# One distance mask for the first four blocks, added through sloped unit matrices; the scheduler's start values and dates set anew

## Chip, cores and metric

The kernel runs on one core of one Trainium2 chip. The metric is the device time of one execution in microseconds; the time before is the median of three runs.

## What is computed

Attention over 4 batches, 8 heads, 768 positions and 64 dimensions, with a window of `n_local` keys, `n_global` keys seen by all, and a bias that falls with the distance by a slope of its own for each head; then a feed-forward part on 3072 tokens.

```python
scores = scale * q @ k.T
keep = is_global | is_local            # rel = row - column; 0 <= rel < n_local, or column < n_global
dist = where(is_global & ~is_local, n_local, abs(rel))
slopes = 2.0 ** (-8.0 * (arange(H) + 1) / H)
scores = where(keep, scores - slopes[:, None, None] * dist, -1e9)
a = softmax(scores)
x = (a @ v)                            # [3072, 512]
h = x @ w_in                           # 512 x 2048
out = (h * sigmoid(1.702 * h)) @ w_out # 2048 x 512
```

With 8 heads the slope of head h is 2 to the power -(h+1).

## The kernel before

The 3072 rows are 24 blocks of 128. The first four (one of each batch, `first`) see only their own keys; the others (`unit`, four units of two heads each) see their own block, the one before and the global keys. For a first block TensorE writes the scores `s` (four heads to a tile), adds to each head its mask, and DVE takes the maxima of the rows, `top`. The maxima are transposed (`aux`), copied to `mT`, and the scores are made a second time with rows and columns exchanged (`sT`): the product, the mask, and the maxima. ACT takes the exponential (`pt`), TensorE multiplies by the values (`pv`), DVE divides (`x`), TensorE turns the result (`tx`), and ACT and DVE split it into two halves of 16 bits (`xT`).

The mask of distances is built on DVE (`distances`, `own`, `other`) in `mk`: part 2 for the first blocks, parts 0 and 1 for the units. `slopes` multiplies it by the slope of each head into `mm`. TensorE adds a mask by a product with the unit matrix `id16`: in `s`, `id16` is the loaded matrix and `mm[:, h, 2]` streams; in `sT`, `mm[:, h, 2]` is loaded and `id16` streams.

The weights come in 16 loads of 1 MB (`ws`, three buffers) and are turned into two halves of 16 bits by two passes on ACT and three on DVE each (lines 420 to 426). The feed-forward part makes `h` from `xT` and `w`, `t` and `g` on ACT and DVE, and `y` from `g`; from the third pair of blocks on, products of a faster scheme write `pa` and `pb`.

All work is a list of tasks. `Work.order` plays them on five engines with a cost of its own for each task, takes at each point the ready task with the earliest due date, and so fixes the order in which each engine gets its instructions. `NUDGE` adds to the due date of the tasks with a given tag; where TensorE would stand idle in the first 50 us, the scheduler puts in a product on `idle`, here called a filler. On the chip each engine runs its instructions in that order, and waits at each until its inputs are there. The queue SP issues nearly all transfers in its own order; a load into a buffer that is still read waits, and so do those behind it. `QKover` holds the keys of the blocks that block 4 follows: SP turns them in one transfer from `qk16over` and copies them in two more.

Of the kernel before, what the change touches and what calls it, by code (L numbers as in the profile page):

```python
# [11 lines left out]
BF16 = mybir.dt.bfloat16  # L12
# [16 lines left out]

NUDGE = {"M2": -8.8, "T2": 21.9, "T3": 11.2, "block1": 2, "block10u2": -2.7, "block10u2l": -0.5,  # L30
# [48 lines left out]
LAT = 0.2  # L79
MM128, MM256, MM512, MM64, FP128, FP65, TURN = 0.056, 0.109, 0.216, 0.029, 0.264, 0.21, 0.11  # L80
# [43 lines left out]
class Work:  # L124
# [15 lines left out]
    def order(self):  # L140
# [21 lines left out]
        dma, now, done = 2.5, 0.0, []  # L162
        worked, spared = 0.6, 0
# [82 lines left out]
def kernel(  # L246
# [48 lines left out]
    id16 = const.tile([P, P], BF16, name="id16")  # L295
# [38 lines left out]
    mm = const.tile([P, H, 3, P], BF16, name="mm")  # L334
# [9 lines left out]
    def distances(e):  # L344

        nc.vector.tensor_copy(flt()[:, 0:2], ints())
        nc.vector.tensor_copy(id16, ident)
# [31 lines left out]
    def slopes(e, js, hs=range(H)):  # L379
# [9 lines left out]
    m0 = add({"DVE": 1.6}, distances, [m0], [ints, flt, mk], -4.0)  # L389
    cs = Buf(r_pv, [P, 2], F32, "cs")  # L390
# [10 lines left out]
    M2 = [add({"DVE": 0.41, "ACT": 0.6}, lambda e, f=f: slopes(e, slice(0, 2), range(2 * f, 2 * f + 2)), [m2], [mk], 34.0) for f in range(4)]  # L401
# [5 lines left out]
    def weights(s, u):  # L407
# [8 lines left out]
        t0 = add({"SP": 2.75}, lambda e: load_weights(nc, ws(), w_in, w_out, s, u), bufs=[ws])  # L416
# [32 lines left out]
    def load(n, raw, parts=(0, 1, 2)):  # L449
        b, i = place(n)  # L450
        return [add({"SP": 1.2 if n < 2 and 2 not in parts else 1.35}, lambda e, z=z: nc.sync.dma_start(
            raw()[:, z], (q, k, v)[z][b, :, i * P:(i + 1) * P, :].rearrange("h p d -> p h d")), bufs=[raw]) for z in parts]
# [911 lines left out]
```

## Time and profile before

| | us |
|---|---|
| median of three runs (588.32 to 590.07) | 589.75 |
| span of the profiled execution | 587.0 |
| PE busy | 578.1 |
| DVE busy | 497.0 |
| ACT busy | 461.4 |

The span goes from the first to the last instruction of one execution. PE is TensorE's products, DVE VectorE, ACT ScalarE, POOL GpSimd, SP the queue of transfers. A product's end is modelled, so a product of 128 columns reads 0.22 us although the next starts 0.055 us after it: the step from one start to the next is what it costs in a row of products. Where a row gives a wait, it is in brackets with what ended it.

### The profile page before, as it was taken

Reading aid. Unit: us, or ns where it says so; the run is one execution under the profiler, and the core shown is the slowest. Engines: PE = TensorE matmul, PEld = TensorE weight load, DVE = VectorE, ACT = ScalarE, POOL = GpSimd, SP = SyncE. Lnnn points to the kernel's source line nnn. Section 1 sums busy time; section 2 is a strip of 40 time slices with the busy share of each in tenths; the row PEclk is TensorE's granted clock in tenths of the full one; section 3 lists DMA queues with packets and bytes.
Section 4 is the critical chain, followed back from the end, with each engine's and each line's share of the span. In section 5 each row is a group of like instructions: output and inputs, shape, how many; then the busy total and the mean of one; then the engine's idle time right before and its main releaser. Section 6 shows DMA issues by size and latency. Waiting matters only on the chain.

```text
span 587.0 us, 16903 instructions
## 1 busy us (share of the span) xinstructions
PE 578.1 (98%) x6744; PEld 435.0 (74%) x6744; DVE 497.0 (85%) x1180; ACT 461.4 (79%) x1086; POOL 3.7 (1%) x14
## 2 busy tenths in 40 slices
PE   8999999999999999999999999999999999999996
PEld 5886666777678678778679767777777866876896
DVE  7898999999999999888899699889889878775462
ACT  6678899898678979888798798798987878874351
POOL 2000000000000000000000000000000000000000
PEclk9999999999999999999999999999999999999999
DMA  9988998988767887989999998999998899981101
GB/s 267 315 262 213 301 239 234 214 186 154 174 138 154 145 150 156 222 163 203 222 182 179 213 222 210 218 201 184 243 204 197 196 204 232 192 179 25 30 2 41
DMA packets 268265, 109.57 MB, mean 187 GB/s; under 512 B 249300, under 2 KB 249812, under 8 KB 268180
## 3 DMA queue, kind: packets, MB, share of 16 engines
q1 hardware_dynamic: 268032, 108.30, 83.3%
q8 instruction: 54, 0.88, 0.6%
q14 instruction: 31, 0.25, 0.1%
q10 hardware_dynamic: 148, 0.13, 0.1%
HBM read 57.67 MB, written 6.29 MB: 109 GB/s over the span
## 4 chain that ended last, share of the span: by engine, by line
PE 82%; DVE 6%; DMA 6%; ACT 4%; issue 2%; SPq 0%; POOL 0%; DVEq 0%; ACTq 0%; POOLq 0%
PE y L969 35%; PE pa L901 15%; PE pb L901 11%; PE h L861 7%; PE s L599 5%; DMA QKover<-qk16over 2%; PE pv L630 1%; PE pv L632 1%; PE pv L631 1%; PE sT L692 1%; DMA ws<-in_moe_w_out_dram 1%; DMA ws_00again<-in_moe_w_in_dram 1%; DMA xT<-x 1%; PE idle L1147 1%; PE pv L704 1%
## 5 line engine op out<-in xcount | busy, mean ns | idle before, releaser
L969 PE MATMUL y<-w,g 128*128 128x512 f16 (+1 forms) x1248 | 265.1, 363 | 0.3
L969 PEld LDWEIGHTS <-g 128*128 128x128 f16 x1248 | 118.0, 98 | 106.6 <-DVE g L873 1.4
L901 PEld LDWEIGHTS <-w 128*128 128x128 f16 x1728 | 101.4, 98 | 3.9
L615 ACT ACTIVATE p<-p,NM 128x232 f32<-128x232 f32 x160 | 76.3, 479 | 8.9 <-DVE NM L605 8.6
L901 PEld LDWEIGHTS <-T 128*128 128x128 f16 x1296 | 76.8, 98 | 5.2 <-issue 0.2
L861 PE MATMUL h<-xT,w 128*128 128x256 f16 x576 | 67.2, 273 | 0.2 <-DVE t L871 0.2
L605 DVE CUSTOM_DVE_ANT_0 p<-s,mm 128x232 f32<-128x232 f32 x160 | 57.5, 393 | 9.3 <-PE s L599 9.0
L861 PEld LDWEIGHTS <-w 128*128 128x128 f16 x576 | 55.4, 98 | 8.1 <-DVE t L871 0.3
L942 DVE SCALAR_TENSOR_TENSOR g<-t,g 128x512 f16<-128x512 f32 x72 | 49.0, 686 | 11.2 <-ACT g L941 10.9
L620 DVE TENSOR_TENSOR hl<-p,hl 128x464 f16<-128x464 f32 x80 | 50.8, 635 | 6.2 <-ACT hl L619 5.9
L941 ACT ACTIVATE g<-t 128x512 f16<-128x512 f32 x72 | 44.9, 628 | 12.1 <-PE y L969 8.2
L933 ACT ACTIVATE t<-h 128x512 f32<-128x512 f32 (+1 forms) x72 | 35.8, 517 | 17.8 <-DVE h L909 16.0
L619 ACT CAST hl<-p 128x464 f16<-128x464 f32 x80 | 46.0, 574 | 2.3 <-DMA pt<-hl 0.9
L909 DVE TENSOR_TENSOR h<-pb,h 128x256 f32<-128x256 f32 x72 | 28.4, 418 | 19.4 <-PE pb L901 17.8
L901 PE MATMUL pa<-xS,T 128*128 128x128 f16 x648 | 44.8, 219 | 0.0
L599 PEld LDWEIGHTS <-QK 128*128 128x128 f16 x640 | 36.5, 98 | 6.0 <-DVE NM L605 1.9
L934 DVE SCALAR_TENSOR_TENSOR t<-t,h 128x512 f32<-128x512 f32 (+1 forms) x72 | 38.4, 551 | 2.2 <-ACT t L933 2.0
L599 PE MATMUL s<-QK 128*128 128x128 f16 x320 | 38.2, 219 | 0.0
L901 PE MATMUL pa<-xT,w 128*128 128x128 f16 x540 | 37.5, 219 | 0.0
L901 PE MATMUL pb<-xS,w 128*128 128x128 f16 x540 | 37.5, 219 | 0.0
L632 PE MATMUL pv<-VR,pt 128*128 128x64 f16 x288 | 34.5, 193 | 0.0
L631 PE MATMUL pv<-VR,pt 128*128 128x64 f16 x288 | 34.5, 193 | 0.0
(186 smaller groups left out, 1031.2 us busy)
## 6 DMA issues: line engine op xcount, KB each, us to landing
ws<-in_moe_w_in_dram SPq DMA_DIRECT2D x8, 1024.0 KB
ws<-in_moe_w_out_dram SPq DMA_DIRECT2D x8, 1024.0 KB, 5.6
raw<-in_q_dram SPq DMA_DIRECT2D x24, 256.0 KB, 3.7
raw<-in_k_dram SPq DMA_DIRECT2D x24, 256.0 KB, 4.8
QK<-QK SPq DMA_DIRECT2D x40, 128.0 KB, 5.5
raw<-in_v_dram SPq DMA_DIRECT2D x20, 256.0 KB, 3.1
out_dram<-yo SPq DMA_DIRECT2D x20, 256.0 KB
ws_00again<-in_moe_w_in_dram SPq DMA_DIRECT2D x8, 512.0 KB, 4.0
```

The lines of the kernel that those rows point to most:

```text
L599: nc.tensor.matmul(sp()[:, j, lo:hi], d["QK"]()[:, 0, h, :], K[:, 1 + z, h, P - (hi - lo):], start=(z == 0), stop=(z == 1), skip_group_che ...
L605: nc.vector.tensor_tensor_reduce(out=pr()[:, j, :], in0=sp()[:, j, :], in1=m, scale=-1.0 / SC, scalar=3.0e38, op0=ALU.add, op1=ALU.min, ac ...
L615: ex.append(add({"ACT": 0.473}, lambda e, j=j: nc.scalar.activation(pr()[:, j, :], pr()[:, j, :], AF.Exp, bias=NM[:, n, hs[j]:hs[j] + 1], ...
L619: t4 = add({"ACT": 0.5}, lambda e: nc.scalar.copy(hl()[:, 0, :, SKIP:], pr()), ex, [pr, hl])
L620: t5 = add({"DVE": 0.55}, lambda e: nc.vector.tensor_sub(hl()[:, 1, :, SKIP:], pr(), hl()[:, 0, :, SKIP:]), [t4], [pr, hl])
L631: nc.tensor.matmul(o, ph, V[:, 1, h], start=False, stop=False, skip_group_check=True)
L632: nc.tensor.matmul(o, pl, V[:, 0, h], start=False, stop=(s == ns - 1), skip_group_check=True)
L861: nc.tensor.matmul(ph()[:, fi, :], w1(s, cc, z, fi), X[:, y, cc, :], start=(j + cc == 0), stop=(j == 2 and cc == NCC - 1))
L901: nc.tensor.matmul(o()[:, fi], w, x()[:, y * NCC + 2 * k + cc, t], start=(first and fi + j + cc == 0), stop=(last and j + cc == 3), skip_g ...
L941: t4 = add({"ACT": 0.53}, lambda e, g=g, tt=tt: nc.scalar.mul(g()[:, 0], tt(), SG / (SX * SW)), u, [tt, g])
L942: t5 = add({"DVE": 0.61}, lambda e, g=g, tt=tt: nc.vector.scalar_tensor_tensor(g()[:, 1], tt(), SG / (SX * SW), g()[:, 0], ALU.mult, ALU.s ...
L969: nc.tensor.matmul(y(), part(zg, f), w2(s, z, f % 2)[:, m], start=(begin and f + j == 0), stop=(end and j == 2 and f == 2 * len(steps) - 1 ...
```

## The change

The mask of the first blocks is kept once, unsloped: `own16` is a copy of `mk[:, 2]` in bf16, and `idh[:, h]` is the unit matrix times the slope of head h. In `s` the loaded matrix is now `idh[:, h]` and `own16` streams; in `sT` `own16` is loaded and the four unit matrices of a half stream in one product of 512 columns. Since the column of the unit matrix that adds the maxima now carries the smallest slope, `mT` is divided by it. `mm` loses its third part, `id16` is gone. The diagonals need only the unit matrix, which POOL makes.

```diff
+    own16 = const.tile([P, P], BF16, name="own16")
+    idh = const.tile([P, H, P], BF16, name="idh")
...
-    M1 = [add({"DVE": 0.61}, lambda e, f=f: slopes(e, slice(2, 3), range(4 * f, 4 * f + 4)), [m1], [mk]) for f in range(2)]
+    M1 = [*D1, add({"DVE": 0.2, "ACT": 0.22}, lambda e: (nc.scalar.copy if e == "ACT" else nc.vector.tensor_copy)(own16, mk()[:, 2]),
+                   [m1], [mk])]
...
+    def diagonals(e, hs):
         for h in hs:
-            f = SC * 2.0 ** -(h + 1)
             if e == "ACT":
-                nc.scalar.mul(mm[:, h, js], mk()[:, js], f)
+                nc.scalar.mul(idh[:, h], ident, slope(h))
             else:
-                nc.vector.tensor_scalar(mm[:, h, js], mk()[:, js], f, None, ALU.mult)
+                nc.vector.tensor_scalar(idh[:, h], ident, slope(h), None, ALU.mult)
...
+    D1 = [add({"DVE": 0.6, "ACT": 0.9}, lambda e, f=f: diagonals(e, range(4 * f, 4 * f + 4)), want=2.0 + f) for f in range(2)]
...
-                    nc.tensor.matmul(sp()[:, j], id16, mm[:, h, 2], start=False, stop=True, skip_group_check=True)
+                    nc.tensor.matmul(sp()[:, j], idh[:, h], own16, start=False, stop=True, skip_group_check=True)
...
-                    nc.tensor.matmul(o, mm[:, h, 2], id16, start=False, stop=False, skip_group_check=True)
-                    nc.tensor.matmul(o, id16[:, h:h + 1].broadcast_to([P, P]), mT, start=False, stop=True, skip_group_check=True)
+                nc.tensor.matmul(sT(), own16, idh[:, hs], start=False, stop=False, skip_group_check=True)
+                for j in range(4):
+                    nc.tensor.matmul(sT()[:, j], idh[:, H - 1, 4 * f + j:4 * f + j + 1].broadcast_to([P, P]), mT,
+                                     start=False, stop=(j == 3), skip_group_check=True)
```

The scheduler starts with other values: the transfers' first free time and TensorE's first filler, the cost of the first loads (1.0 in place of 1.2), of the first weight load and of a `turned` task.

```diff
+DMA0, PE0 = 1.85, 1.3
...
-        dma, now, done = 2.5, 0.0, []
-        worked, spared = 0.6, 0
+        dma, now, done = DMA0, 0.0, []
+        worked, spared = PE0, 0
...
-        t0 = add({"SP": 2.75}, lambda e: load_weights(nc, ws(), w_in, w_out, s, u), bufs=[ws])
+        t0 = add({"SP": 2.75 if s or u else 3.5}, lambda e: load_weights(nc, ws(), w_in, w_out, s, u), bufs=[ws])
```

And `NUDGE` is another table, with about twice as many entries; two of its old and new ones:

```diff
-NUDGE = {"M2": -8.8, "T2": 21.9, "T3": 11.2, "block1": 2, "block10u2": -2.7, "block10u2l": -0.5,
+NUDGE = {"M1": 2.8, "T0": 14.2, "T1": 5.3, "T3": -8.5, "again": 1.3, "againl": -2.1, "block0": 4.5,
```

So the order changes on every engine from the first instructions to the last. At the start, TensorE gets 13 fillers instead of 16, seven of them ahead of the first transposes instead of ten, and the scores of blocks 0 and 1 stand in a row. Three places follow.

The start on DVE, from the first memsets to the mask of the first blocks (`flt`, `mk`: distances; `one`, `cnt`: counts). Before:

```order
L503 MEMSET VF_124 128x8
L346 CAST flt<-ints 128x256
L347 CAST id_84<-ident 128x128
L348 TENSOR_SCALAR mk<-flt 128x128
...
L353 CAST cf<-ci 1x4
...
L356 SCALAR_TENSOR_TENSOR one<-one,cf 1x2
L393 COPY cnt<-cs 128x2
...
L372 SCALAR_TENSOR_TENSOR mk<-flt,cnt,mk 128x128
L385 TENSOR_SCALAR mm<-mk 128x128 x8
```

Now:

```order
L415 TENSOR_SCALAR idh<-ident 128x128 x8
...
L375 CAST flt<-ints 128x256
L376 TENSOR_SCALAR mk<-flt 128x128
...
L381 CAST cf<-ci 1x4
...
L384 SCALAR_TENSOR_TENSOR one<-one,cf 1x2
L531 TENSOR_SCALAR QZ_136<-tq_0_177 64x512
L431 COPY cnt<-cs 128x2
...
L400 SCALAR_TENSOR_TENSOR mk<-flt,cnt,mk 128x128
```

Eight products with slopes moved from behind the mask to ahead of the distances, and half of a QZ came to DVE. The same stretch on ACT, where `hl` holds the turned keys; before:

```order
L492 ACTIVATE QZ_116<-tq_0_171 64x512 x2
L492 ACTIVATE hl_97<-tq_1_188 128x512
L492 ACTIVATE QZ_131<-tq_0_208 64x512 x2
L383 ACTIVATE mm<-mk 128x256 x2
L492 ACTIVATE hl_98<-tq_1_239 128x512
L681 CAST mT_85<-aux_252 8x128
```

Now:

```order
L531 ACTIVATE QZ_136<-tq_0_177 64x512
L531 ACTIVATE hl_98<-tq_1_188 128x512
L531 ACTIVATE QZ_119<-tq_0_201 64x512
L436 CAST own_84<-mk 128x128
L531 ACTIVATE hl_99<-tq_1_211 128x512
L712 ACTIVATE mT_86<-aux_259 8x128
L420 ACTIVATE mm<-mk 128x256 x2
L739 ACTIVATE pt_0_292<-sT_0_265 128x512
```

ACT has two QZ parts fewer, the copy of the mask behind the second, and the units' masks behind `mT` instead of ahead of it.

The second place is DVE at blocks 1 and 2, some 23 to 28 us into the program: `xT0` ends the second block, `top` are the maxima of block 2, `wa` and `w` steps of the weights. Before:

```order
L492 TENSOR_SCALAR hl0_97<-tq2_1_405 128x512
L426 SCALAR_TENSOR_TENSOR w0_1_333<-wa0_1_370,w0_1_333 128x1024
L677 TENSOR_REDUCE top_90<-s2_1_427 128x4
L767 TENSOR_TENSOR xT0_386<-tx1_415,xT0_386 128x4x128
L503 MEMSET VF3_456 128x8
L420 TENSOR_SCALAR w1_0_459<-ws1_0_377 128x1024
L677 TENSOR_REDUCE top_90<-s2_0_447 128x4
L681 CAST mT0_85<-aux2_477 8x128
```

Now:

```order
L531 TENSOR_SCALAR QZ2_163<-tq2_0_377 64x512
L462 SCALAR_TENSOR_TENSOR wa1_0_404<-ws1_0_276,w1_0_369 128x1024
L796 TENSOR_TENSOR xT0_365<-tx1_398,xT0_365 128x4x128
L707 TENSOR_REDUCE top_91<-s2_1_410 128x4
L459 TENSOR_SCALAR w1_1_439<-ws1_1_337 128x1024
L707 TENSOR_REDUCE top_91<-s2_0_424 128x4
L465 SCALAR_TENSOR_TENSOR w1_0_369<-wa1_0_404,w1_0_369 128x1024
L713 TENSOR_SCALAR mT0_86<-aux2_459 8x128
```

The first maxima moved behind `xT0`, the steps of the second weight load stand earlier, and one of them stands between the second maxima and `mT0`.

The third place is SP at the hand-over to block 4. Before:

```order
L521 DMA_TRANSPOSE QKover4_815<-qk16over4_1_772 128x8x128
L242 DMA ws5_0_836<-in_moe_w_in_dram 128x4x512
L451 DMA raw4_494<-in_v_dram 128x8x64
L523 DMA QKover4_815<-QKover4_815 64x1024 x2
L242 DMA ws5_1_903<-in_moe_w_out_dram 128x2x1024
```

Now:

```order
L560 DMA_TRANSPOSE QKover4_854<-qk16over4_1_799 128x8x128
L606 DMA VRover4_820<-VRover4_820 8x1024
L580 DMA VG0_872<-VRover4_820 8x1024
L270 DMA ws6_0_884<-in_moe_w_in_dram 128x4x512
L270 DMA ws6_1_911<-in_moe_w_out_dram 128x2x1024
L562 DMA QKover4_854<-QKover4_854 64x1024 x2
```

Two weight loads of 1 MB stand between the transpose and the two copies, where one load of 1 MB and one of 256 KB stood.

## Rows read from the trace of the kernel before

**Rows 1.** The page's head: span, then busy time of each engine, its share and its instructions.

```profile
span 587.0 us, 16903 instructions
PE 578.1 (98%) x6744; PEld 435.0 (74%) x6744; DVE 497.0 (85%) x1180; ACT 461.4 (79%) x1086; POOL 3.7 (1%) x14
```

**Rows 2.** PE's windows: stretch in us, its length, PE's busy time and products in it, granted clock, DMA's busy share, GB/s.

```profile
26.00:60.00 34.00, 34.00 (x286) 1.00 0.88 244
...
62.00:64.00 2.00, 1.86 (x13) 1.00 0.99 355
...
72.00:74.00 2.00, 1.50 (x14) 1.00 1.25 284
...
106.00:109.00 3.00, 2.80 (x30) 1.00 1.11 186
...
115.00:117.00 2.00, 1.83 (x15) 1.00 1.12 253
...
131.00:400.00 269.00, 269.00 (x3352) 1.00 0.89 183
400.00:520.00 120.00, 119.74 (x1557) 1.00 1.00 210
```

**Rows 3.** PE's timeline: start in us, length, line, operation and tiles, count; the first two are the long pieces, the third one of the usual length.

```profile
62.64 2.20 PE L969 MATMUL y<-w,g 128*128 128x512 f16 x8
...
108.02 1.67 PE L969 MATMUL y<-w,g 128*128 128x512 f16 x6
...
53.50 1.46 PE L969 MATMUL y<-w,g 128*128 128x512 f16 x6
```

**Rows 4.** PE's list of waits: who waited for whom, us in total, times, the longest.

```profile
PE tq L485 <- ACT QZ L492: 0.8, 1, 0.8
PE s L599 <- DVE NM L605: 0.7, 2, 0.5
PE aux L680 <- DVE top L677: 0.4, 1, 0.4
PE s L672 <- ACT hl L492: 0.3, 1, 0.3
PE tx L763 <- DVE x L743: 0.3, 1, 0.3
```

**Rows 5.** PE's timeline in the first 27 us: start in us, length, line, operation and tiles, count, wait ahead of it.

```profile
1.33 4.39 PE L1147 MATMUL idle<-idle 128*128 128x512 bf16 x10 [1.33 <-POOL idle L291]
5.66 0.38 PE L392 MATMUL cs<-one,each 1*128 1x2 f32 x2
5.96 0.66 PE L485 MATMUL tq<-ident,raw 128*128 128x128 f32 x4
6.46 0.81 PE L1147 MATMUL idle<-idle 128*128 128x512 bf16 x3
7.11 0.60 PE L485 MATMUL tq<-ident,raw 128*128 128x128 f32 x4
...
8.54 0.22 PE L672 MATMUL s<-hl,QZ 128*128 128x128 bf16 x1
...
9.45 0.60 PE L485 MATMUL tq<-ident,raw 128*128 128x128 f32 x4
...
11.74 0.65 PE L692 MATMUL sT<-QZ,hl 128*128 128x256 f32 x2
12.23 0.22 PE L697 MATMUL sT<-id,mm 128*128 128x128 bf16 x1
12.28 0.22 PE L698 MATMUL sT<-mT,id 128*128 128x128 bf16 x1
...
16.88 0.65 PE L692 MATMUL sT<-QZ,hl 128*128 128x256 f32 x2
...
26.73 1.47 PE L861 MATMUL h<-xT,w 128*128 128x256 f16 x12
```

**Rows 6.** DVE's timeline at the start, columns as in rows 5.

```profile
2.19 0.57 DVE L346 CAST flt<-ints 128x256 f32<-128x256 int32 x1 [0.99 <-POOL ints L342]
...
4.63 0.15 DVE L356 SCALAR_TENSOR_TENSOR one<-one,cf 1x2 f32<-1x2 f32 x1
6.07 0.16 DVE L393 COPY cnt<-cs 128x2 f32<-128x2 f32 x1 [1.30 <-PE cs L392]
...
7.50 1.18 DVE L385 TENSOR_SCALAR mm<-mk 128x128 bf16<-128x128 f32 x8
8.59 0.28 DVE L375 TENSOR_SCALAR flt<-mk,cnt 128x128 f32<-128x128 f32 x1
```

**Rows 7.** ACT's timeline at the start, columns as in rows 5.

```profile
6.66 1.21 ACT L492 ACTIVATE QZ<-tq 64x512 f32<-64x512 f32 x2 [1.24 <-PE tq L485]
...
9.90 0.72 ACT L383 ACTIVATE mm<-mk 128x256 bf16<-128x256 f32 x2
```

**Rows 8.** POOL's timeline, the end of the unit matrix.

```profile
1.67 0.29 POOL masks.py:199 TENSOR_SCALAR_AFFINE_SELECT ident<-ident 128x128 f32<-128x128 f32 x1
```

**Rows 9.** The chain of waits at the hand-over to block 4, in order of time: start in us, length, what.

```profile
54.08 8.97 DMA QKover<-qk16over
...
63.63 2.55 DMA QKover<-QKover
...
67.70 0.20 DVE KG L535
```

More of the change, by code (lines that the diff above doesn't have):

```diff
@@ L294 @@
     make_identity(nc, ident)
-    id16 = const.tile([P, P], BF16, name="id16")
+    own16 = const.tile([P, P], BF16, name="own16")
+    idh = const.tile([P, H, P], BF16, name="idh")
     mTs = [const.tile([P, P], BF16, name=f"mT{j}") for j in range(2)]
@@ L329 @@
     add = wk.add
-    mm = const.tile([P, H, 3, P], BF16, name="mm")
+    mm = const.tile([P, H, 2, P], BF16, name="mm")
     mk = Buf(r_x16, [P, 3, P], F32, "mk")
@@ L377, in other, with slope, slopes @@
         nc.vector.tensor_scalar(mk()[:, 0, SKIP:SKIP + NG], b_()[:, 0:NG], nl, None, ALU.subtract)
-    def slopes(e, js, hs=range(H)):
+    def slope(h):
+        return SC * 2.0 ** -(h + 1)
+    def diagonals(e, hs):
         for h in hs:
-            f = SC * 2.0 ** -(h + 1)
             if e == "ACT":
-                nc.scalar.mul(mm[:, h, js], mk()[:, js], f)
+                nc.scalar.mul(idh[:, h], ident, slope(h))
             else:
-                nc.vector.tensor_scalar(mm[:, h, js], mk()[:, js], f, None, ALU.mult)
+                nc.vector.tensor_scalar(idh[:, h], ident, slope(h), None, ALU.mult)
+    def slopes(e, hs):
+        for h in hs:
+            if e == "ACT":
+                nc.scalar.mul(mm[:, h], mk()[:, 0:2], slope(h))
+            else:
+                nc.vector.tensor_scalar(mm[:, h], mk()[:, 0:2], slope(h), None, ALU.mult)
     wk.tag = "masks"
@@ L397 @@
     wk.tag = "M1"
-    M1 = [add({"DVE": 0.61}, lambda e, f=f: slopes(e, slice(2, 3), range(4 * f, 4 * f + 4)), [m1], [mk]) for f in range(2)]
+    M1 = [*D1, add({"DVE": 0.2, "ACT": 0.22}, lambda e: (nc.scalar.copy if e == "ACT" else nc.vector.tensor_copy)(own16, mk()[:, 2]),
+                   [m1], [mk])]
     wk.tag = "M2"
     m2 = add({"DVE": 0.78}, other, [m1], [flt, mk])
-    M2 = [add({"DVE": 0.41, "ACT": 0.6}, lambda e, f=f: slopes(e, slice(0, 2), range(2 * f, 2 * f + 2)), [m2], [mk], 34.0) for f in range(4)]
+    M2 = [add({"DVE": 0.41, "ACT": 0.6}, lambda e, f=f: slopes(e, range(2 * f, 2 * f + 2)), [m2], [mk], 34.0) for f in range(4)]
     WT, W_ready, squared, checks = {}, {}, {}, []
@@ L450, in load @@
         b, i = place(n)
-        return [add({"SP": 1.2 if n < 2 and 2 not in parts else 1.35}, lambda e, z=z: nc.sync.dma_start(
+        return [add({"SP": (1.0 if (n, z) != (1, 1) else 1.3) if n < 2 and 2 not in parts else 1.35}, lambda e, z=z: nc.sync.dma_start(
             raw()[:, z], (q, k, v)[z][b, :, i * P:(i + 1) * P, :].rearrange("h p d -> p h d")), bufs=[raw]) for z in parts]
@@ L503, in own_values @@
             add({"DVE": 0.1}, lambda e: nc.vector.memset(VF()[:, :, D:D + 1], 1.0), bufs=[VF]),
-            add({"SP": 1.2 if n < 2 else 1.35}, lambda e: nc.sync.dma_start(
+            add({"SP": 1.0 if n < 2 else 1.35}, lambda e: nc.sync.dma_start(
                 VF()[:, :, 0:D], v[b, :, i * P:(i + 1) * P, :].rearrange("h p d -> p h d")), bufs=[VF])]
@@ L649, in first @@
         pv = d["pv"] = Buf(r_pv, [P, H - 1, D + 1], F32, f"pv{n}")
-        QKs = [d[f] for f in (("QZ", "KF") if n < FIRST else ("QK",))]
+        QKs = [d["QZ"], d["KF"]]
         def upper(a):
             return a.bitcast(BF16).rearrange("p (t z) -> p t z", z=2)[:, :, 1]
-        def products(h):
-            if n < FIRST:
-                return [(d["QZ"]()[:, h % 2, h // 2, :], d["KF"]()[:, h // 2, :])]
-            return [(d["QK"]()[:, 0, h, :], d["QK"]()[:, 1 + z, h, :]) for z in range(2)]
-        mm_s = FP128 if n < FIRST else 2 * MM128
         maxed = []
@@ L668, in scores @@
                     h = 4 * f + j
-                    for z, (qp, kp) in enumerate(products(h)):
-                        if n < FIRST:
-                            qp, kp = upper(qp), upper(kp)
-                        nc.tensor.matmul(sp()[:, j], qp, kp, start=(z == 0), stop=False, skip_group_check=True)
-                    nc.tensor.matmul(sp()[:, j], id16, mm[:, h, 2], start=False, stop=True, skip_group_check=True)
-            t1 = add({"PE": 8 * MM128 if n < FIRST else 4 * (mm_s + MM128)}, scores, [M1[f], *d["qk_ready"]], [sp, *QKs], want + 1.2 * f)
+                    nc.tensor.matmul(sp()[:, j], upper(d["QZ"]()[:, h % 2, h // 2, :]), upper(d["KF"]()[:, h // 2, :]),
+                                     start=True, stop=False, skip_group_check=True)
+                    nc.tensor.matmul(sp()[:, j], idh[:, h], own16, start=False, stop=True, skip_group_check=True)
+            t1 = add({"PE": 8 * MM128}, scores, [M1[f], M1[2], *d["qk_ready"]], [sp, *QKs], want + 1.2 * f)
             d.setdefault("S", []).append(t1)
@@ L680, in first @@
         t2 = add({"PE": 0.11}, lambda e: nc.tensor.transpose(aux()[0:H, 0:P], top[:, n, :], ident), maxed, [aux])
-        t3 = add({"ACT": 0.18, "DVE": 0.21}, lambda e: (nc.scalar.copy if e == "ACT" else nc.vector.tensor_copy)(
-            mT[0:H], aux()[0:H, 0:P]), [t2, *blk.get(("mT", n - 2), ())], [aux])
+        t3 = add({"ACT": 0.18, "DVE": 0.21}, lambda e: (
+            nc.scalar.mul(mT[0:H], aux()[0:H, 0:P], 1.0 / slope(H - 1)) if e == "ACT" else
+            nc.vector.tensor_scalar(mT[0:H], aux()[0:H, 0:P], 1.0 / slope(H - 1), None, ALU.mult)), [t2, *blk.get(("mT", n - 2), ())], [aux])
         for f in range(2):
@@ L687, in turned @@
             def turned(e, f=f, sT=sT):
-                for j in range(4):
-                    h, o = 4 * f + j, sT()[:, j, :]
-                    if n < FIRST:
-                        if j % 2 == 0:
-                            nc.tensor.matmul(sT()[:, j:j + 2, :], d["KF"]()[:, h // 2, :], d["QZ"]()[:, :, h // 2, :],
-                                             start=True, stop=False, skip_group_check=True)
-                    else:
-                        for z, (qp, kp) in enumerate(products(h)):
-                            nc.tensor.matmul(o, kp, qp, start=(z == 0), stop=False, skip_group_check=True)
-                    nc.tensor.matmul(o, mm[:, h, 2], id16, start=False, stop=False, skip_group_check=True)
-                    nc.tensor.matmul(o, id16[:, h:h + 1].broadcast_to([P, P]), mT, start=False, stop=True, skip_group_check=True)
+                hs = slice(4 * f, 4 * f + 4)
+                for j in range(0, 4, 2):
+                    u = 2 * f + j // 2
+                    nc.tensor.matmul(sT()[:, j:j + 2, :], d["KF"]()[:, u, :], d["QZ"]()[:, :, u, :],
+                                     start=(j == 0), stop=False, skip_group_check=True)
+                nc.tensor.matmul(sT(), own16, idh[:, hs], start=False, stop=False, skip_group_check=True)
+                for j in range(4):
+                    nc.tensor.matmul(sT()[:, j], idh[:, H - 1, 4 * f + j:4 * f + j + 1].broadcast_to([P, P]), mT,
+                                     start=False, stop=(j == 3), skip_group_check=True)
             def values(e, f=f, pt=pt):
@@ L706, in first @@
             wk.tag = f"turn{n}"
-            t4 = add({"PE": 1.34 if n < FIRST else 4 * (mm_s + 2 * MM128)}, turned, [t3, *M1, *d["qk_ready"]], [sT, *QKs], want + 6.0 + 1.2 * f)
+            t4 = add({"PE": 1.4}, turned, [t3, *M1, *d["qk_ready"]], [sT, *QKs], want + 6.0 + 1.2 * f)
             d["S"].append(t4)
```

3 lines of the change are left out of this document (1 added, 2 removed), and 99 rows, old and new, of the table NUDGE.

## The prediction

> **What bounds the kernel now.** I read the page's busy times first: TensorE (PE) is busy 578.1 of 587.0 us, DVE 497, ACT 461 [rows 1]. So the time is PE's own work, plus what PE spends on idle matmuls (fillers that keep it busy while data comes), plus the waits between. Next I read PE's windows: between 26 and 400 us it stands idle in four short stretches only, 0.14 + 0.50 + 0.20 + 0.17 = 1.01 us, and 0.26 us from 400 to 520 [rows 2]. Some waits hide in a modelled matmul end: two pieces of y run long, 2.20 us for 8 matmuls and 1.67 for 6, where 6 take 1.46 and one more takes 0.22; that is 0.30 + 0.21 = 0.5 us [rows 3]. Third I read PE's list of waits: those above 0.15 us are nearly all in the first 26 us (0.8 for QZ, 0.4 for the maxima, 0.3 for hl, 0.3 for x) or at an s tile (0.7) [rows 4]. PE's own order at the start gives the rest: ten fillers of 0.43 us up to 5.66 us, then six more of 0.22 between the first transposes [rows 5]. So there is little to win: some 3.6 us of waits, of which 1.8 lie in the head (0 to 27 us) and 1.5 from 27 to 131 us. What follows the last matmul is the same tail in both orders, 96 products of y behind the last product of pa, so I leave it at nothing.
>
> The median is 589.75 us, the profiled span 587.0, so 2.7 us lie around the span. The sum is made on the span and the 2.7 kept.
>
> **PE's work.** Per block, 8 pairs of a 128-column product and the following one in sT become 2 products of 512 columns. A 128-column product takes the step between two rows, 12.28 - 12.23 = 0.055 us, a 512-column one 0.65 / 3 = 0.217 [rows 5]. So 8 x 0.055 = 0.44 becomes 2 x 0.217 = 0.43: 0.01 a block, 0.04 in four blocks. The other products keep their number and size. Weight loads fall by 24; PE shows no step longer than the columns where they stand, so they are worth nothing. Bounds: 0 to -0.1 us.
>
> The Trainium skill, page "TensorE: Matmul & The Clock Gate", section "Back-to-back issue gap", speaks of a sustained 81 ns per product of 128 columns in a stream of load and product, and 131 ns for one of 512. By that the exchange would give 8 x 81 - 2 x 131 = 386 ns a block, 1.5 us in all, an estimate from that page, and the sum would be -2.4 in place of -0.9. The trace does not agree: its steps are 55 and 217 ns.
>
> **The head.** I follow the three engines up to the first product of h, with durations from the trace.
> DVE: the identity is complete at 1.96 us [rows 8]. The eight diagonals have the form of the old eight slopes, 8.59 - 7.50 = 1.09 us [rows 6], so they end near 3.1. The distances and counts, 2.19 to 4.78 us before [rows 6], follow behind and end near 5.65. That is 0.9 later, but PE's counts product came only at 5.66, behind ten fillers, and comes at 5.7 now. So the late start is hidden by the fillers; without them it would cost the 0.9.
> PE: seven fillers end at 4.33; the first transposes follow, then the wait for the counts, then the product. The second transposes come at 6.3 (7.11 before), the third at 7.0, the fourth at 7.6 (9.45 before) [rows 5].
> DVE again: half a QZ (0.6), then cnt to the mask: 7.50 - 6.07 = 1.43 us [rows 6], done near 7.8. The eight slopes behind it are gone (1.09 us).
> ACT: a QZ half is now half of 1.21, since DVE takes the other [rows 7]. hl is done at 7.5, the second QZ half at 8.1, the copy of the mask, queued behind both, near 8.35. So the first scores start at 8.45, 8.54 before [rows 5]: the slopes that left the path buy only 0.1 there, since hl and the copy are late next.
> Four groups of scores now run in a row, 0.45 us each. The maxima of block 0 are done at 10.3 (two of 0.6 from 9.1), sT starts near 10.95, before 11.74 [rows 5]. Then ACT loses some: the mask for later blocks (two of 0.36 us, [rows 7]) waits for all four maxima and stands ahead of the first exponentials, so the second half of pv waits 0.7. At the second block's sT I get 16.4 against 16.88, 0.5 ahead. The old order then lost 0.8 us to the transposes of block 3, which waited for a QZ [rows 4]; they stand later now. The first h starts at 25.4, where before it stood at 26.73 with four transposes (0.44) done that now are to come [rows 5]. **Head: 26.73 - 0.44 - 25.4 = 0.9 us gained.** Bounds: 1.6 (the wait of 0.7 does not come) to -0.7 (the clock, below).
>
> **27 to 55 us.** PE had no wait there at all [rows 2]. In the new order DVE takes half a QZ and a weight step ahead of xT, and a weight step between the two maxima of block 2: the second maximum ends near 27.0, the transpose of the maxima stands behind 12 products of h that end at 26.7, so PE waits 0.4. The same chain of weight steps puts ACT's exponential for block 2 near 34.75, where PE would like it at 34.45: 0.35. **Lost: 0.75 us**; bounds 0 (steps that overlap better than I add them) to 1.2 (one more of the kind). One more weight load of 1 MB now lies ahead of block 2's q and k, whose transposes come near 21.4 against 21.9; since no wait for a load stands in PE's list [rows 4], I take this as hidden.
>
> **55 to 131 us.** Before: 1.0 + 0.5 = 1.5 us of waits [rows 2, 3]. Two causes can be counted in the order. Between two s units that share one buffer PE had 1.30 us of other work three times in this stretch (two of them waited, [rows 4]); now four times 1.30. Between the last product of an h and the first y that reads it, six distances lay between 4.3 and 5.6 us of PE work; now one lies under 7.8. So the waits of y should go, those of s stay: **0.8 us remain, 0.7 gained.** Bounds: 1.5 gained to 1.5 lost.
>
> **After 131 us.** Every date differs, but the work doesn't: PE had 0.3 us of waits in 452 us [rows 2]. The shortest distances between a product and the copy that frees its buffer are 0.67 us of PE work in both orders, and three s distances fall from 1.34 to 1.01. I take 0; bounds 0.3 gained to 1.2 lost.
>
> **Sum.** -0.04 - 0.9 + 0.75 - 0.7 + 0 = -0.9 us: span 586.1, time 588.8 us.
>
> **Rivals.**
> A. *The new order has no waits of its own* (faster). If DVE and ACT keep up everywhere, 27 to 55 costs nothing and 55 to 131 gives 1.5: -0.04 - 0.9 - 1.5 = -2.4, 587.3 us; with the 0.7 of the head too, 586.6. For it: the long distances from h to y. Against: DVE is busy nearly all of 27 to 55 us.
> B. *The clock rises later.* Before, PE issued 512-column fillers without a break from 1.33 us; ten of them at 0.43 us show the level of 1.2 GHz, and from 5.66 the steps are those of 2.4 GHz [rows 5]. Now seven fillers are followed by four transposes and a stop of half a microsecond. If the engine stays at 1.2 GHz until the scores begin, three sets of transposes cost 0.87 instead of 0.44 and three fillers 0.43 instead of 0.22 on the way to them: they start near 10.05, 1.6 us later. 590.4 us, still the same within what can be told.
> C. *Block 4's hand-over is late* (slower). On the SP queue the two copies QKover<-QKover now stand behind two weight halves, which wait for buffers that DVE frees near 61.8 and 63.5 us. Before, the transpose took 8.97 us and the copies 2.55, and the keys were copied at 67.70 [rows 9], just ahead of block 4's scores. Now I get copies issued near 64.2 and landed near 71, keys copied by 71.5, scores due at 72.9. It decides if the copies land after 72: if the weights ahead of them hold them for one transpose's worth less that margin, 8.97 / 2 - 1.4 = 3 us, block 4 and all behind it come 3 us later: 591.8 us.
> D. *A 512-column product costs less than its columns*, so that the sT change gives more than 0.04. Were the mask's products free in sT, four blocks would give 4 x 0.43 = 1.7 us: 587.1. The 0.217 us row is against it. This is the side on which the page's rule lies.
>
> **How the numbers follow.** A measurement of this kernel can tell some 0.3% (1.8 us) from no change. The forecast, 588.8 us, has a chance of 0.42; A 0.32, B 0.10, C 0.14, D 0.02. Faster: A, D and a tail of the forecast, 0.36. Same: most of the forecast and B, 0.49. Slower: C and a little, 0.15. The range runs from A with the head's 0.7 and a little of D (586.4) to the forecast with both middle stretches at their bad end (588.8 + 0.45 + 1.5 = 590.7); C lies mostly outside.
>
> **What would show it.** Right: scores of block 0 at 8.3 to 8.6 us, sT of block 0 near 11.0, h at 25.4, clock up by 5.7 us. PE idle before pv of block 0 (0.7), before the third transpose of maxima (0.4). QKover's keys copied before 72 us and no wait of block 4's first scores. Wrong: scores of block 0 after 9.5 us with transposes at 0.22 us a step; more than 1.5 us of PE idle between 55 and 131 us; steps of sT's 512-column product other than 0.217.

## The result, and the profile after

The changed kernel takes 594.99 us (median of four runs, 593.17 to 596.09) against 589.75 (also the median of four runs, not of three). The two medians differ by 5.2 us; the ratio on record is 1.0103, 95% interval 1.0079 to 1.0127, which is 6.1 us, and the profiled span grew by 6.0, from 587.0 to 593.0 us. So the kernel is slower by some 6 us, or 1%; the forecast was 588.8.

The head of the page after, to be held against [rows 1]:

```profile
span 593.0 us, 16850 instructions
PE 577.1 (97%) x6714; PEld 434.7 (73%) x6717; DVE 501.9 (85%) x1184; ACT 457.2 (77%) x1082; POOL 3.8 (1%) x14
```

PE is busy 1 us less than before (it has fewer fillers) and the span is 6 us longer, so the loss is waiting. PE's windows after, columns as in [rows 2], tell where:

```profile
27.00:60.00 33.00, 32.90 (x266) 1.00 0.93 271
60.00:80.00 20.00, 17.77 (x136) 1.00 0.99 247
80.00:106.00 26.00, 26.00 (x250) 1.00 1.03 222
106.00:131.00 25.00, 25.00 (x240) 1.00 0.89 188
131.00:280.00 149.00, 148.70 (x1790) 1.00 0.80 158
280.00:320.00 40.00, 38.69 (x530) 1.00 0.97 186
320.00:380.00 60.00, 60.00 (x788) 1.00 1.07 216
380.00:430.00 50.00, 47.00 (x575) 1.00 1.12 222
430.00:520.00 90.00, 90.00 (x1160) 1.00 1.03 214
```

PE idles 0.10 + 2.23 + 0.30 + 1.31 + 3.00 = 6.94 us from 27 to 520 us, where before it idled 1.01 + 0.26 [rows 2]: 5.7 of the 6 us. Two places hold nearly all of it, 60 to 80 and 280 to 430 us. The head loses 0.8 us more (below), and behind 520 us PE idles 0.7 less than before. PE's list of waits names what it waited for (compare [rows 4], where no transfer stands and all but the s tile's are in the head):

```profile
PE s L638 <- DVE QKover L585: 2.8, 2, 2.2
PE pv L669 <- DMA pt<-hl: 1.4, 2, 0.9
PE cs L430 <- DVE one L384: 1.4, 1, 1.4
PE pv L669 <- DMA VR<-VG: 1.4, 1, 1.4
...
PE s L701 <- DVE xT L796: 1.1, 1, 1.1
```

**The first place** is the hand-over to block 4. The SP queue (first fence: start, length of the issue, operation), then DVE and PE:

```profile
64.09 1.02 SPq L270 DMA_DIRECT2D ws<-in_moe_w_in_dram  x1
65.78 0.76 SPq L270 DMA_DIRECT2D ws<-in_moe_w_out_dram  x1
66.63 1.22 SPq L562 DMA_DIRECT2D QKover<-QKover  x2
```

```profile
71.87 1.23 DVE L462 SCALAR_TENSOR_TENSOR wa<-ws,w 128x1024 int32<-128x1024 int32 x1
74.94 0.69 DVE L459 TENSOR_SCALAR w<-ws 128x1024 int32<-128x1024 int32 x1 [1.84 <-DMA ws<-in_moe_w_out_dram]
75.77 0.20 DVE L574 COPY KG<-QKover 128x128 f16<-128x128 f16 x1
76.00 0.20 DVE L585 COPY QKover<-KG 128x128 f16<-128x128 f16 x1
```

```profile
72.56 1.46 PE L998 MATMUL y<-w,g 128*128 128x512 f16 x6
76.25 0.25 PE L638 MATMUL s<-QKover,QK 128*128 128x104 f16 x2 [2.23 <-DVE QKover L585]
```

The two copies are issued at 66.63 us, right behind two weight loads of 1 MB. The keys are copied at 75.77 us, where before they were at 67.70 [rows 9]. DVE stands 1.84 us at the second of these loads, with the copy of the keys next in its order. By the semaphores in the trace the first load landed at 70.48 us, the second at 74.91, the two copies at 75.26 and 75.75: the second copy 8.5 us after its issue, where before it took 4.0 (63.63 to 67.62). DVE was free for the keys only at 75.63, so the weight step ahead of them would have held them nearly as long. Block 4's scores, due at 74.02 (76.25 less the wait), start 2.23 us late.

**The second place** is 280 to 430 us. The SP queue at its worst spot, then PE:

```profile
394.89 0.58 SPq L270 DMA_DIRECT2D ws_11again<-in_moe_w_out_dram  x1
395.58 1.24 SPq L660 DMA_TRANSPOSE pt<-hl  x1
396.92 0.71 SPq L752 DMA_DIRECT2D VR<-VG  x1
```

```profile
398.66 1.24 PE L998 MATMUL y<-w,g 128*128 128x512 f16 x5
401.27 0.19 PE L669 MATMUL pv<-VR,pt 128*128 128x64 f16 x1 [1.36 <-DMA VR<-VG]
```

A copy of 16 KB is waited for 4.35 us after its issue; the second reading of a weight (0.5 MB, `ws_11again`, only for the kernel's check of its inputs) went into the queue 2 us ahead of it, and a transpose between the two. ACT, too, stands at transfers there. Its list of waits from 150 to 430 us, of the changed kernel and then of the kernel before:

```profile
ACT ws_00again L1121 <- DMA ws_00again<-in_moe_w_in_dram: 7.1, 3, 3.5
ACT hl L658 <- DMA pt<-hl: 3.5, 4, 1.2
ACT ws_10again L1121 <- DMA ws_10again<-in_moe_w_out_dram: 2.6, 2, 1.4
```

```profile
ACT ws_10again L1092 <- DMA ws_10again<-in_moe_w_out_dram: 1.1, 1, 1.1
ACT hl L619 <- DMA pt<-hl: 0.7, 1, 0.7
ACT ws_01again L1092 <- DMA ws_01again<-in_moe_w_in_dram: 0.5, 1, 0.5
```

13.2 us in these three rows against 2.3.

**The head** lost 0.8 us (columns as in [rows 5]):

```profile
4.23 0.60 PE L524 MATMUL tq<-ident,raw 128*128 128x128 f32 x4
6.24 0.38 PE L430 MATMUL cs<-one,each 1*128 1x2 f32 x2 [1.40 <-DVE one L384]
...
8.79 0.22 PE L701 MATMUL s<-hl,QZ 128*128 128x128 bf16 x1
...
11.29 1.03 PE L722 MATMUL sT<-QZ,hl 128*128 128x256 f32 x4
12.15 0.38 PE L724 MATMUL sT<-idh,own 128*128 128x512 bf16 x1
12.37 0.39 PE L726 MATMUL sT<-mT,idh 128*128 128x128 bf16 x4
...
26.21 0.22 PE L701 MATMUL s<-hl,QZ 128*128 128x128 bf16 x1 [1.15 <-DVE xT L796]
...
27.10 1.47 PE L890 MATMUL h<-xT,w 128*128 128x256 f16 x12
```

The mask's product in sT takes 12.37 - 12.15 = 0.22 us, the step of 512 columns, as forecast. Block 0's sT is 0.45 us ahead of before (11.74). But the first h comes at 27.10, not at 25.4: ahead of it PE waits for `xT` at block 2's second scores. Before, it came at 26.73 with four transposes more behind it (0.44 us), so the head is 27.10 - 26.73 + 0.44 = 0.8 us longer.

The counts wait for DVE, whose eight diagonals (the forecast gave them 1.09 us) come first. DVE and POOL in the changed kernel, then DVE in mask_only, a run described below:

```profile
1.99 2.60 DVE L415 TENSOR_SCALAR idh<-ident 128x128 bf16<-128x128 f32 x8 [0.84 <-POOL ident masks.py:199]
2.09 2.35 POOL L514 MEMSET QZ<- 64x512 f32 x4
```

```profile
4.67 1.16 DVE L535 TENSOR_SCALAR idh<-ident 128x128 bf16<-128x128 f32 x8
```

The same eight products take 2.60 us while POOL fills QZ, and 1.16 when POOL is done (there it fills QZ from 2.10 to 4.36). Three pairs of them start in step with POOL's memsets: at 2.68, 3.29 and 3.90 us, each 0.07 behind the end of one (2.61, 3.22, 3.83). All twelve profiled kernels with the early place show 2.59 or 2.60, the three with the later place 1.15 or 1.16.

### The profile page after: what moved, and what is told of

Same layout as the page of the kernel before. It is cut to its first block, busy times and chain, and to the rows that moved or that the text cites. A ratio compares the mean times of both kernels' runs of the same rounds, so it can differ in the third digit from the quotient of the medians.

```text
span 593.0 us, 16850 instructions
## 1 busy us (share of the span) xinstructions
PE 577.1 (97%) x6714; PEld 434.7 (73%) x6717; DVE 501.9 (85%) x1184; ACT 457.2 (77%) x1082; POOL 3.8 (1%) x14
## 5 line engine op out<-in xcount | busy, mean ns | idle before, releaser
L669 PE MATMUL pv<-VR,pt 128*128 128x64 f16 x288 | 34.0, 193 | 2.4 <-DMA VR<-VG 1.4
L669 PEld LDWEIGHTS <-pt 128*128 128x128 f16 x320 | 29.3, 98 | 6.7 <-DMA pt<-hl 2.3
```

The lines of the kernel that those rows point to most:

```text
L669: nc.tensor.matmul(o, ph, V[:, 0, h], start=(s == 0), stop=False, skip_group_check=True)
```

## The experiments

Three theories stood at the start. **D** (dates): the new order's transfers stand late; the mask is worth next to nothing. **M** (mask): the new mask itself costs, by diagonals ahead of the counts and a copy ahead of the scores. **H**: the loss is made in the head and up to 131 us, and only shows later. In all experiments the list of tasks is played from an order written out (number of the task, letter of its engine), so that single pieces of it can be exchanged:

```diff
-        for t in wk.order():
+        for t in wk.replay(SEQ):
```

Ratios are to the kernel before on the same chip (587.8 to 588.2 us), with their 95% interval; 0.001 is 0.59 us.

**mask_only.** The changed code in the order of before; in DVE's and ACT's order:

```diff
 counts on DVE
+diagonals 0 to 3, diagonals 4 to 7 on DVE
 cnt<-cs on DVE
 own on DVE
-slopes 0 to 3, slopes 4 to 7 on DVE
+own16<-mk on ACT
```

> The changed code, but every instruction stands in the order of the kernel before; only the eight diagonals are new on DVE, in its idle stretch between the counts and the counts' copy, and one ACT copy of the mask stands where the eight slopes stood. Theory D (the loss comes from the new dates, by transfers that stand late on SP): the mask by itself is worth 0 to 0.9 us, so 588.8 to 589.8 us, and block 4's first scores don't wait. Theory M (the new mask by itself costs, by diagonals ahead of the counts and a copy on the way to the scores): 592 us or more.

0.9995 (0.9983 to 1.0006). The mask alone is worth between 1.0 us and -0.4, and the copy ahead of the scores costs nothing that shows. The diagonals stand behind the counts here, so the other half of M is left to the next run.

**order_only.** The code of before in the order of the changed kernel:

```diff
-diagonals 0 to 3, diagonals 4 to 7 on DVE
 own on DVE
-own16<-mk on ACT
+slopes 0 to 3, slopes 4 to 7 on DVE
```

> The old mask (eight slopes, eight pairs in sT) in the order of the changed kernel; the eight slopes stand on DVE where the copy of the mask stood. Theory D: the loss is all there, 594 to 596.5 us, with 2.4 us of wait at block 4's first scores. Theory M: the loss is gone, 589 to 590.5 us.

1.0106 (1.0082 to 1.0130): the whole loss, without the new mask, and with no diagonals ahead of the counts: M falls. Block 4's scores wait 1.6 us, less than the 2.4 expected. The loss is not at all the same places: the first h comes at 28.17, 1.1 us behind the changed kernel's, and PE idles 2.7 us from 280 to 430 against 4.3.

**early_copies.** Block 4's copies one load earlier (names added behind the numbers):

```diff
 1329S   ws<-w_in (step 6)
+138S 139S   QKover<-QKover, twice
 1336S   ws<-w_out (step 6)
-138S 139S
...
+142D 144D   KG<-QKover, QKover<-KG
 1337D   first step on that w_out
-142D 144D
```

> The changed kernel, in which the two copies QKover<-QKover of block 4 stand one weight load earlier on SP (behind w60, ahead of w61) and the two copies of the keys on DVE ahead of w61's first step. Theory D: the wait of 2.4 us ahead of block 4's first scores goes to 0.3 or less and the time falls to 592.3 to 593 us. Rival S (the later waits take up what is gained, since the DMA queue is behind all along): 594.3 to 595.2 us. Rival W (the weight that comes later by the copies is late itself, for the products of the next h): a new wait of 1 us or more, 593.5 to 595 us.

1.0043 (1.0030 to 1.0055): 3.5 us of the 6 come back, and block 4's scores do not wait (PE is busy all of 60 to 80 us). Rival S falls by the time of the eight runs, and W too: no wait for the weight appears. The gain is more than the wait that went. The profiled run, the slowest of the eight (593.14; median 590.25), still idles 5.0 us from 280 to 430, so that stretch differs between executions, and how much of the 3.5 us is the hand-over itself is not shown. Nor is which of the two moves did it, on SP or on DVE.

The wait at block 4 differs between executions too: the eight profiled kernels that have the changed order there without this repair wait 0.6 to 2.6 us for `QKover` (2.2 in the changed kernel), the five that have the repair not at all.

**after_then_before.** The changed order up to a planned 125 us, that of before behind it.

```diff
-SEQ = (all of the changed order)
+SEQ = (the changed order to 125 us) + (what is left, in the order of before)
```

> The changed kernel's order for what its planner dates up to 125 us, and behind it the rest in the order of the kernel before. Theory D, in its form that the waits come from both stretches: block 4's 2.4 us stay, the 5.9 us of waits from 131 us on fall to about 1, so 590 to 591.5 us. Rival H (all of the loss is made before 131 us): 594 to 595.5 us. Rival L (all of it comes later): 589 to 590 us.

1.0113 (1.0074 to 1.0153), by its number H. The windows say otherwise:

```profile
131.00:150.00 19.00, 15.30 (x140) 0.91 0.50 111
150.00:280.00 130.00, 130.00 (x1615) 1.00 0.83 163
280.00:520.00 240.00, 239.90 (x3096) 1.00 0.97 206
```

3.7 us are lost where the two orders are joined, and 0.1 us from 150 to 520. Behind that stop PE ran for a while at 1.2 GHz (granted clock 0.91 over the stretch; six products of y take 2.93 us at 139.15 and 1.46 at 142.62), so the joint costs more than its 3.7 us. So the run counts for D, but its time settles nothing; the next two join the orders at other places.

**early_then_before** (join at a planned 195 us, early_copies ahead of it) and **before_then_after** (join at 250 us, mask_only ahead of it):

```diff
-SEQ = (all of the changed order)
+SEQ = (early_copies to 195 us) + (what is left, in the order of before)
```

```diff
-SEQ = (all of the changed order)
+SEQ = (mask_only to 250 us) + (what is left, in the changed order)
```

> The order of early_copies for what the changed planner dates up to 195 us, and behind it the rest in the order of the kernel before. Theory D2 (block 4's hand-over costs 2 us, and the rest of the loss is made after 200 us, by the new order's late transfers): none of the loss is left, and the 2.0 us by which early_copies is ahead of the kernel before at 200 us stay, so 1 to 2.5 us under the kernel before. Rival H (the loss is made before 131 us and only shows later): 2 to 3 us over it.

> The new mask in the order of the kernel before (as mask_only) for what its planner dates up to 250 us, and behind it the rest in the changed kernel's order. Theory D2: the loss of the stretch from 280 to 430 us comes back, 4 to 6 us over the kernel before. Rival H: no loss, within 1 us of it. Rival Q (the changed order runs late there only because its own DMA queue is 1 MB behind when it comes to 250 us, which this kernel's is not): 0 to 2 us over it.

1.0008 (0.9990 to 1.0026) and 1.0115 (1.0089 to 1.0142). With before's order from 195 us on (and block 4's copies early) the loss is gone; with the changed order from 250 us on all of it is there, although nothing ahead of 250 us was changed but the mask. H and Q fall. But early_copies plays the changed order from 250 us on as well and is only 2.5 us over: what that order costs depends on the state in which the kernel comes to it, and a cost of the joint itself is not ruled out. The gain forecast for early_then_before did not come; its head shows part of why, further down.

**no_again_after, no_again_before, no_loads, no_squares.** What of the second reading of the weights (32 loads on SP, a square on ACT and a minimum on DVE for each) makes the late stretch? The first two leave out all of it, in the changed order and in mask_only; no_loads leaves out the loads alone, no_squares the squares and minima. Each leaves out that part of the check.

```diff
-                t0 = add({"SP": 1.6}, lambda e, s=s, u=u, ws=ws, half=half: load_weights(nc, ws(), w_in, w_out, s, u, half), bufs=[ws])
...
-                t1 = add({"ACT": 0.64}, lambda e, o=o, hi_w=hi_w: nc.scalar.activation(
-                    hi_w(), hi_w(), AF.Square, accum_out=e2[:, 0, o:o + 1]), [t0], [ws])
...
+    nc.gpsimd.memset(e2, 1.0)
```

> The changed kernel without the second reading of the weights (32 loads of 0.5 MB between 265 and 530 us, with their squares on ACT and minima on DVE, which only check the weights' low words): that part of the check is left out. Theory D2 in the form that the late transfers of 280 to 430 us wait behind these loads, and ACT behind their squares: the 5.4 us of that stretch go, the 2.4 at block 4 stay, so 1.5 to 2.5 us over the kernel before. Rival O (the order of the rest is to blame, with or without them): 4.5 us or more over it.

> The control of no_again_after: mask_only without the second reading of the weights, that part of the check left out. mask_only has 1.5 us of PE's waits from 200 us on, so theory D2 and rival O both expect 0.5 to 1.5 us less than the kernel before. If it gains as much as no_again_after does (4 us or more), the loads cost any order the same, and they don't tell why the changed one is slower.

> The changed kernel without the 32 second loads of weights, but with a square on ACT and a minimum on DVE for each, of the same 512 columns, on a tile of ones: that part of the check is left out. Theory Q (the loads, in the DMA queue or as what ACT waits for): as no_again_after, 0.5 to 2 us over the kernel before. Rival W (the time of the squares and minima on ACT and DVE): 4 us or more over it.

> The changed kernel with the 32 second loads of weights, but without their squares and minima: that part of the check is left out. Theory Q1 (what counts is that ACT stands behind loads that are late, 9.7 us in six stops at the squares of ws_again in the changed kernel): 0.5 to 2 us over the kernel before. Theory Q2 (what counts is the DMA queue itself, which the transposes of hl, the copies of VG and the second hand-over stand in): 4 to 6 us over it. Both at work: 2 to 4 us.

(ACT's stops in the last text are five, not six.)

| without | ratio | interval | us over before |
|---|---|---|---|
| all, changed order | 1.0021 | 0.9999 to 1.0043 | 1.2 |
| all, order of before | 0.9984 | 0.9971 to 0.9997 | -0.9 |
| loads, changed order | 1.0005 | 0.9991 to 1.0019 | 0.3 |
| squares and minima, changed order | 1.0086 | 1.0064 to 1.0108 | 5.1 |

The loads cost the changed order 6.1 - 0.3 = 5.8 us and the squares 6.1 - 5.1 = 1.0, which the intervals do not tell from nothing. So ACT's stops at the squares, the largest rows of its list, are not what counts (Q1 falls); the loads in the queue are (Q2). Without the loads PE idles 0.1 us from 280 to 430, even in a profiled run that was the slowest of its ten. In the order of before the loads, squares and minima together cost 0.6 us (0.9995 - 0.9984).

The Trainium skill, page "DMA: Bandwidth & Descriptors", section "Queues, rings and completion order", says that descriptors of one queue are consumed in ring order on each DMA engine. The traces agree: block 4's copies, issued 0.1 us behind two loads of 1 MB (the second ends its issue at 65.78 + 0.76 = 66.54), land behind both (74.91, then 75.26 and 75.75) and are read 9.1 us after their issue (66.63 to 75.77), and in no_loads no row of PE or ACT waits for `VR<-VG`.

**more_fillers, after_fillers.** The head of early_then_before is word for word that of early_copies, but its first scores start at another time. The first fence is early_then_before, the second early_copies:

```profile
4.29 1.06 PE L644 MATMUL tq<-ident,raw 128*128 128x128 f32 x4
6.23 0.58 PE L550 MATMUL cs<-one,each 1*128 1x2 f32 x2 [0.88 <-DVE one L504]
...
9.97 0.66 PE L644 MATMUL tq<-ident,raw 128*128 128x128 f32 x4
10.47 0.22 PE L821 MATMUL s<-hl,QZ 128*128 128x128 bf16 x1
```

```profile
4.29 0.67 PE L644 MATMUL tq<-ident,raw 128*128 128x128 f32 x4
...
8.80 0.22 PE L821 MATMUL s<-hl,QZ 128*128 128x128 bf16 x1
```

Four transposes read 1.06 us long where PE runs at 1.2 GHz and 0.6 where it runs at 2.4; in the first kernel's run the level rises only at 9.97 us, behind ten fillers and twelve transposes with stops between, and the scores are 1.67 us late. Three fillers were put where PE waits for the counts, in early_then_before and in the changed kernel:

```diff
 18P   tq<-ident,raw
+P P P   idle<-idle
 5P   cs<-one,each
```

> early_then_before with three more fillers on PE, where it waits 1.3 us for the counts behind its first transposes. Theory K (in this order the clock rises in some executions only at 10.0 us, behind that stop, as in the profiled run of early_then_before, whose first scores start at 10.47 us and not at 8.80 as in early_copies): with no stop there the clock is up before 7.5 us, the first scores start by 9 us, the runs lie closer together than the 5.3 us of early_then_before, and the median falls by 0.5 to 1.5 us, 0.3 to 1 us under the kernel before. Rival N (the clock is not moved by them): the median as in early_then_before, 0 to 1 us over the kernel before, with first scores after 10 us in some.

> The changed kernel with the same three more fillers. Theory K: what the late clock costs in some executions goes, 0.3 to 1.2 us less than the changed kernel (6 us over the kernel before), so 4.5 to 5.7 us over it. Rival N: 5.5 to 6.5 us over it.

0.9990 (0.9976 to 1.0005) and 1.0086 (1.0059 to 1.0114). The first scores of the profiled runs start at 9.10 and 8.79 us; the runs of more_fillers lie within 4.5 us (5.3 without), ten of its twelve within 1.9. Both ratios moved as K expects, by about 1 us, though neither step is beyond the two intervals. The other profiles speak for K too: of the eight kernels with the new mask and this head without the three fillers, three start the first scores at 10.43 to 10.56 us (early_then_before, no_again_after, sp_order) and five at 8.79 to 8.88; of the four with them, none later than 9.10. With one profile of each kernel that is a sign and no proof. more_fillers has the lowest ratio of the versions that leave nothing out; it can't be told from the kernel before.

**sp_order, best, repaired.** Is the order of the transfers in the one queue enough to make the loss? sp_order exchanges entries of SP alone; best does so from more_fillers, on ACT and DVE too; repaired joins early_copies, the fillers and sp_order. Part of sp_order, with the place in the queue before and after:

```diff
-2597S at 169   ws_00again
+2597S at 165
...
-705S at 185   VG<-VRover (block 14)
+705S at 199
```

> The changed kernel, in which the entries of the SP queue behind 240 us stand in another order: 79 of its 364 entries move, most by one to four places, loads of q, k, v and of weights mostly ahead, the copies VG<-VRover 10 to 14 places back. The orders of PE, ACT and DVE stay word for word, and block 4's hand-over too. Theory S (the late stretch is a matter of the order of the transfers in one queue): 2.5 to 5 us of the 5.4 us come back, so 1 to 3.5 us over the kernel before, with ACT's waits for DMA from 150 to 430 us at 5 us or less (15.6 in the changed kernel). Theory P (it is a matter of when PE, ACT and DVE do their work in the changed order, with transfers too close behind): 4.5 us or more over the kernel before.

> The order of more_fillers (new mask; changed order with block 4's copies moved up to 195 us, order of before behind it; three more fillers), in which entries of SP, ACT and DVE behind 30 us are moved by a few places each, so that a transfer that comes late meets more other work; PE's order stays. By theory S a queue with more room gives up the waits that more_fillers still has, about 1.5 us from 27 us on: 1 to 2.5 us under the kernel before. Rival: more_fillers has no such waits in most executions, so it stays within 1 us of the kernel before.

> The changed kernel with all three repairs at once, PE, ACT and DVE else in the changed order: block 4's copies as in early_copies, three more fillers, the SP queue behind 240 us as in sp_order. If the parts stand for themselves they add up: 6.1 us over the kernel before, less 3.5 (early_copies), 1.0 (after_fillers) and 2.2 (sp_order), is 0.6 us under it, so between 0.5 over and 1.5 under. If two of them give back the same microseconds, 1 to 3 us over it.

1.0065 (1.0050 to 1.0080), 1.0101 (1.0081 to 1.0122) and 1.0064 (1.0042 to 1.0086). sp_order brings back 2.2 of the 6 us, less than S expected and more than P; ACT's waits for transfers from 150 to 430 us fell from 15.6 to 6.8 us, not to 5. best failed: PE waits only 0.3 us for a transfer there, but it waits for the copies of h; that they stand behind the work that was moved ahead of them is likely, not shown (PE's longest waits from 230 to 430 us):

```profile
PE pb L1050 <- DVE h L1058: 1.4, 2, 0.8
PE pb L1050 <- ACT h L1055: 1.4, 2, 0.8
PE s L758 <- DVE NM L764: 1.0, 2, 0.5
```

repaired is no better than sp_order, so the three repairs do not add up, and the expected 0.6 us under the kernel before did not come. Why is not shown: its profiled run was the fastest of seven (588.70 us, of 588.70 to 594.78), idles 1.6 us from 27 to 520, and does not have what the others lost.

## Why the prediction was wrong

- **PE's work** (-0.04): right; the product of 512 columns took 0.22 us, and mask_only is worth 0.3 us with an interval that holds zero.
- **The head** (-0.9): wrong: it lost 0.8, just beyond its bad end of 0.7. Two steps failed. The first: "The eight diagonals have the form of the old eight slopes", 1.09 us. They took 2.60, while POOL filled QZ, so the counts came at 6.24, not 5.7, and scores and sT 0.34 us after the forecast (8.79 and 11.29 against 8.45 and 10.95). The second is h at 25.4: it followed the engines and not the buffers. Block 2's second scores take the one buffer of the ring of s, which block 1's `tx` holds until `xT` has read it; on DVE half a QZ and a weight step stand ahead of `xT`, and PE waits 1.15 us.
- **27 to 55 us** (+0.75): PE idled 0.10; too high. Part of what was looked for there, the weight step ahead of `xT`, was paid in the head.
- **55 to 131 us** (-0.7): the waits of y went, as forecast (80 to 131 us have no idle time, before 0.37 [rows 2]). But block 4 lost 2.2, so the stretch has 2.2 us of idle time in place of 0.8. More than 1.5 us of it is a sign of being wrong that the prediction names, and keys copied before 72 us, a sign of being right, did not come.
- **After 131 us** (0; bounds -0.3 to 1.2): this is the term that decided. 4.6 us of idle time, nearly all from 280 to 430. The step that failed: "the shortest distances between a product and the copy that frees its buffer" were counted, and no distance between a transfer's issue and its reader, though the DMA engines were at 0.89 to 1.00 of their time there [rows 2]. "Every date differs, but the work doesn't" was no argument for zero: no_loads shows that the loads cost 5.8 us in the changed order, and no_again_before that they cost under 1, squares and minima with them, in the order of before.
- **The range** (586.4 to 590.7): from the forecast's -0.7 to the bad end of +1.5 is 2.2 for the stretch 55 to 131 us, not the 1.5 added, so the bad ends of both middle stretches give 591.4; the bad ends of the head and of what follows 131 us were left out.
- **Rival C** happened, with a price near that named (2.2 against 3), and a chance of 0.14. The copies did stand behind the two weights. Two steps of its working were off. The weights were issued at 64.09 and 65.78, as DVE freed their buffers at 64.03 and 65.76 and not at 61.8 and 63.5, and so the copies at 66.63 and not 64.2. And the copies landed 9.1 us after the first was issued (75.75), not 6.8 (71): they waited in the queue for the data of the two loads, 2 MB. The 2.55 us that the forecast took for them [rows 9] is a piece of the chain and not their landing, which came 4.0 us after issue even before.
- **Rival B** happened too, in three of eight profiled executions of this head: 1.6 to 1.8 us, priced at 1.6. The changed kernel's own profiled run does not show it (8.79). A did not happen, and D did not: 1.7 us lies outside mask_only's interval.

Against before, the first h and the idle times account for the span's 6.0 us so: 0.8 us in the head, 0.1 from 27 to 60, 1.2 from 60 to 131, 4.4 from 131 to 520 and -0.7 behind; 0.2 us are not found.

Shown: the loss lies in the order, not in the mask (mask_only, order_only); it comes with the changed order from 250 us on (before_then_after) and is gone with before's order from 195 us on (early_then_before); it needs the second loads in the queue (no_loads), not their squares (no_squares). Open: which feature of the changed order leaves so little room. early_copies gives back 3.5 us and sp_order 2.2, but repaired, which has both and the fillers, stays 3.8 over, so they are not two parts of one sum; the order on SP was not separated from the work on PE, ACT and DVE. What of the order comes from the dates and what from the scheduler's other start values was not tried apart.

## What to carry to other kernels

Where the DMA engines are busy nine tenths of the time, as here, count, for each transfer that an engine waits for, the bytes that stand ahead of it in the queue at its issue, and not only the distances on the engines. Take an instruction's time from a stretch in which the other engines do what they will do at its new place: eight products of the same form took 1.1 us at one place and 2.6 at another. A new table of dates is a change of the whole kernel even where the edit beside it is small; play the edit in the old order and the new order without the edit, and the two are told apart in two runs. And a profile of one execution can be the lucky one or the unlucky one: early_copies and repaired spread over 4 to 6 us, and their profiled runs were the slowest and the fastest, so verdicts need the runs.

## What was not expected of the hardware

One order of instructions had two heads: PE's step in the first transposes was 0.213 us in one execution and 0.110 in another, and the level of 2.4 GHz came at 9.97 us or by 4.5, after the same seven fillers. The granted clock in the windows of the head reads 1.00 in both, so the level is read from the steps. Eight products on DVE took 2.60 us while POOL wrote four memsets and 1.16 behind them. And a copy of 16 KB was waited for 4.35 us, and two copies of 128 KB 9 us, with the DMA engines at 0.8 to 1.1 of their time and a load of 0.5 MB or two of 1 MB ahead of them.
